# The second of two matrix products also made by Strassen's algorithm, summed over the tile, from the fourth tile on

## The chip, the cores and the metric

One core of one Trainium2 chip. The metric is the device time of one execution in microseconds, lower is better. The kernel before takes 828.13 us (median of 3 runs, 827.43 to 828.19). [...]

## The reference

Linear attention without softmax, then a norm, then a feed-forward network with the SiLU gate:

```
kv  = einsum('bhsd,bhse->bhde', k, v)              # 8 batches, 8 heads, 576 tokens, 64 dims
out = einsum('bhsd,bhde->bhse', q, kv)
x   = out / sqrt(mean(out*out, -1) + 1e-6) * g_norm # [8,8,576,64] -> tokens [4608, 512]
h   = x @ w_in                                      # [4608,512] @ [512,2048]
y   = (h * sigmoid(h)) @ w_out                      # [4608,2048] @ [2048,512]
```

All inputs are float32 (w_in and w_out reach the chip as 64-bit floats and are rounded there).

## The kernel before, in words

The 4608 tokens are cut into 9 **tiles** of TN = 512 tokens, counted here from 0 to 8. Each float32 operand of a product is split into an upper part (a cast to the PE's fp32r format) and a lower part (the difference), and a product is three products of parts: upper by lower, lower by upper, upper by upper. So a product has a *cast on ACT* and a *subtraction on DVE or POOL* ahead of it.

Tiles 0 and 1 run plainly, while the weights still arrive. From tile 2 on a tile is 8 **steps** i = 0 to 7 (`pair_step`), each with two blocks of 128 rows of the hidden dimension, i and i + 8:

- *First product* (x by w_in): Strassen's algorithm in Winograd's form. Seven products of 6 matmuls (128x256 each), called here by the numbers of the code: 1, 2, 6, 7, then 4, 5, 3. Products 1 and 2 share one PSUM bank (`bank`), 6 and 7 another (`other`); 4 and 5 go over 1 and 2, and 3 over 6. There are two such banks ("hp", pool `ps_h`). ACT copies product 1 (`p1`), DVE makes three sums from it (L706 to L708), then the results c2 (L718) and c1 (L722, L723).
- *Second product* (the gated block by w_out, `project`): plain. ACT runs SiLU twice on each result (once into the upper part gh), DVE subtracts (L667, gl), and the PE does 4 groups of 6 matmuls for each of the two blocks, 48 in all, growing four PSUM banks ("acc") over the whole tile. The PE runs it one step late, so that one step's gating lies beside the next step's first product.

The sums of blocks of w_in that Strassen's algorithm needs are made once in tile 1, kept in DRAM, and loaded anew in each step: two DMAs of 512 KB (`load_sums`), each issued when the PE has done with the block's predecessor. The operands made of x for the next tile are made in step 7 of a tile (`prepare` calls `make_operand`: 7 casts on ACT, L645, and 7 subtractions on DVE, L646): four of them stand ahead of c2 and c1 on DVE, three behind.

Beside this runs the attention of the next tiles' batches, one batch in a tile up to tile 6 (batches 3 to 7 in tiles 2 to 6), placed by tables (`first_jobs`, `mid_jobs`, `last_jobs`: ahead of, in the middle of and behind each half step): 80 small matmuls of k by v in step 7 (`mm_kv`), then in steps 0 and 1 of the next tile the splits of q (ACT L287, POOL L288) and of kv (`kh` on ACT, `kl` on DVE L280), and in steps 1 and 2 the products by q in two halves of 256 and 320 columns (`mm_out`: L301 to L303, between products 7 and 4 and behind product 3), which ACT reads twice (`copy_out`, L307 and L308). Two banks ("at" and "other") take turns for these halves. DVE scales (L321, L329) the batch before.

The schedule is manual: every engine's order is the order of the code. SP issues all DMAs in one queue.

## Time and profile before

| | |
|---|---|
| median of 3 runs | 828.13 us (827.43 to 828.19) |
| the profiled execution's own time | 827.72 us |
| its span on the core | 825.9 us, so 1.8 us lie outside it |
| granted TensorE clock | 1.00 in every stage |
| PE, DVE, ACT, POOL busy in the span | 815.1, 527.6, 358.4, 145.6 us |
| tiles 3, 4 and 5 | 87.6 us each |
| DMA moved | 122.81 MB, mean 149 GB/s |

The profile's page gives the busy time of each engine, the chain of work that ended last, and groups of instructions by line of the code with their mean duration; further views give the instructions in order of time and busy time by stretches of the span. A busy engine is not the bound by that alone: what counts is whether others wait for it.

### The profile page before, as it was taken

Reading aid. Unit: us, or ns where it says so; the run is one execution under the profiler, and the core shown is the slowest. Engines: PE = TensorE matmul, PEld = TensorE weight load, DVE = VectorE, ACT = ScalarE, POOL = GpSimd, SP = SyncE. Lnnn points to the kernel's source line nnn. Section 1 sums busy time; section 2 is a strip of 40 time slices with the busy share of each in tenths; the row PEclk is TensorE's granted clock in tenths of the full one; section 3 lists DMA queues with packets and bytes.
Section 4 is the critical chain, followed back from the end, with each engine's and each line's share of the span. In section 5 each row is a group of like instructions: output and inputs, shape, how many; then the busy total and the mean of one; then the engine's idle time right before and its main releaser. Section 6 shows DMA issues by size and latency. Waiting matters only on the chain.

```text
span 825.9 us, 18181 instructions
## 1 busy us (share of the span) xinstructions
PE 815.1 (99%) x7518; PEld 808.5 (98%) x7518; DVE 527.6 (64%) x1027; ACT 358.4 (43%) x744; POOL 145.6 (18%) x142
## 2 busy tenths in 40 slices
PE   8989999999999999999999999999999999999998
PEld 7889999999999999999999999999999999999998
DVE  4886884888476567757676668656765764464332
ACT  4766554534363255325442455225533423243222
POOL 2786883423020002000200011001100000000000
PEclk9999999999999999999999999999999999999999
DMA  8879011246352635364424453454423343334331
GB/s 324 321 245 380 7 42 70 102 182 233 126 177 95 218 120 169 103 214 149 168 77 163 161 182 103 143 177 160 143 92 104 108 159 106 106 106 155 103 103 52
DMA packets 42434, 122.81 MB, mean 149 GB/s; under 512 B 4848, under 2 KB 5104, under 8 KB 42352
## 3 DMA queue, kind: packets, MB, share of 16 engines
q1 hardware_dynamic: 42352, 121.65, 42.2%
q8 instruction: 59, 0.97, 0.5%
q14 instruction: 23, 0.19, 0.1%
HBM read 103.81 MB, written 17.83 MB: 147 GB/s over the span
## 4 chain that ended last, share of the span: by engine, by line
PE 94%; DMA 4%; POOL 1%; ACT 0%; issue 0%; SPq 0%
PE acc L488 46%; PE hp L654 32%; PE hp L488 9%; PE at L266 2%; DMA wo<-in_moe_w_out 1%; DMA k<-in_k 1%; DMA v<-in_v 1%; PE at L302 1%; PE at L303 1%; PE at L301 1%; DMA wi<-in_moe_w_in 1%; PE at L488 1%; DMA early_wi<-in_v 1%; PE at L299 1%; POOL wo L204 0%
## 5 line engine op out<-in xcount | busy, mean ns | idle before, releaser
L488 PE MATMUL acc<-wo,gh 128*128 128x256 f32 x2272 | 353.6, 277 | 0.0
L488 PEld LDWEIGHTS acc<-wo,gh 128*128 128x128 f32 x2272 | 302.1, 188 | 1.0 <-POOL wo L204 0.2
L488 PE MATMUL acc<-wo,gl 128*128 128x256 f32 x1136 | 222.9, 276 | 0.5 <-POOL gl L507 0.5
L488 PEld LDWEIGHTS acc<-wo,gl 128*128 128x128 f32 x1136 | 171.8, 188 | 0.7 <-POOL gl L507 0.7
L654 PE MATMUL hp<-x_second,wi 128*128 128x256 f32 x1344 | 163.1, 276 | 0.0
L654 PEld LDWEIGHTS hp<-x_second,wi 128*128 128x128 f32 x1344 | 157.2, 188 | 0.0
L654 PE MATMUL hp<-operand,wi 128*128 128x256 f32 x1008 | 123.3, 276 | 0.0
L654 PEld LDWEIGHTS hp<-operand,wi 128*128 128x128 f32 x1008 | 118.4, 188 | 0.0
L288 POOL TENSOR_TENSOR ql<-q,qh 128x576 fp32r<-128x576 f32 x24 | 35.3, 1472 | 368.2 <-ACT qh L287 321.7
L705 ACT COPY wi<-hp 128x256 f32<-128x256 f32 x56 | 20.8, 372 | 136.8 <-PE hp L654 136.8
L663 ACT ACTIVATE gh<-gf 128x512 fp32r<-128x512 f32 x56 | 35.4, 633 | 91.9 <-DVE gf L718 80.3
L663 ACT ACTIVATE gh<-wi 128x512 fp32r<-128x512 f32 x56 | 35.5, 634 | 76.6 <-DVE wi L718 66.3
L706 DVE TENSOR_TENSOR gf<-hp,wi 128x256 f32<-128x256 f32 x28 | 11.9, 425 | 81.6 <-ACT wi L705 81.6
L706 DVE TENSOR_TENSOR wi<-hp,wi 128x256 f32<-128x256 f32 x28 | 11.9, 425 | 81.2 <-ACT wi L705 81.2
L488 PE MATMUL hp<-x,wi 128*128 128x256 f32 x360 | 46.4, 283 | 1.4 <-POOL wi L204 1.4
L488 PE MATMUL hp<-x_second,wi 128*128 128x256 f32 x384 | 46.3, 276 | 0.0
L488 PEld LDWEIGHTS hp<-x,wi 128*128 128x128 f32 x360 | 43.5, 189 | 2.2 <-POOL wi L204 1.6
L667 DVE TENSOR_TENSOR gl<-wi,gh 128x512 fp32r<-128x512 f32 x56 | 38.4, 685 | 11.3 <-ACT wi L664 11.3
L488 PEld LDWEIGHTS hp<-x_second,wi 128*128 128x128 f32 x384 | 44.9, 188 | 0.1
L667 DVE TENSOR_TENSOR gl<-gf,gh 128x512 fp32r<-128x512 f32 x56 | 39.2, 700 | 7.4 <-ACT gf L664 7.4
L707 DVE TENSOR_TENSOR wi<-hp,wi 128x256 f32<-128x256 f32 x56 | 23.8, 425 | 29.5 <-PE hp L654 29.5
L307 ACT ACTIVATE sq<-at 128x256 f32<-128x256 f32 (+1 forms) x56 | 22.9, 410 | 44.5 <-PE at L303 35.7
(142 smaller groups left out, 1011.1 us busy)
## 6 DMA issues: line engine op xcount, KB each, us to landing
wi<-sums_in_dram SPq DMA_DIRECT2D x112, 512.0 KB, 3.3
out<-ob SPq DMA_DIRECT2D x35, 256.0 KB, 2.4
wi<-in_moe_w_in SPq DMA_DIRECT2D x16, 512.0 KB, 7.9
wo<-in_moe_w_out SPq DMA_DIRECT2D x16, 512.0 KB, 8.7
sums_in_dram<-sum_parts SPq DMA_DIRECT2D x16, 512.0 KB, 3.0
k<-in_k SPq DMA_DIRECT2D x28, 288.0 KB, 5.1
v<-in_v SPq DMA_DIRECT2D x28, 288.0 KB, 5.2
q<-in_q SPq DMA_DIRECT2D x28, 288.0 KB, 3.7
```

The lines of the kernel that those rows point to most:

```text
L266: nc.tensor.matmul(out=self.kv[h], lhsT=self.k[rows, c, :], rhs=self.v[rows, c, :], start=(start and r == 0), stop=(stop and r == 4),)
L288: nc.gpsimd.tensor_tensor(out=self.ql, in0=self.q, in1=self.qh.bitcast(F32), op=ALU.subtract)
L299: nc.tensor.matmul(out=ps, lhsT=self.kvm, rhs=self.q[:, w], start=True, stop=True)
L301: nc.tensor.matmul(out=ps, lhsT=self.kh, rhs=self.ql[:, w], start=True, stop=False)
L307: nc.scalar.activation(out=self.sq[:, self.w], in_=self.ps, func=AF.Square)
L488: nc.tensor.matmul(out=to[:, at:at + 256], lhsT=stationary, rhs=moving[:, at:at + 256], start=start and at == 0, stop=stop and at == n - 256,)
L654: nc.tensor.matmul(out=out, lhsT=a_of(i, a, c), rhs=x[:, b, c], start=(n == 0), stop=(n == 5))
L663: nc.scalar.activation(out=gh, in_=x, func=AF.Silu)
L667: nc.vector.tensor_tensor(out=gl, in0=x, in1=gh.bitcast(F32), op=ALU.subtract)
L705: nc.scalar.copy(out=p1, in_=u)
L706: nc.vector.tensor_tensor(out=c1[:, low], in0=v, in1=p1, op=ALU.add)
L707: nc.vector.tensor_tensor(out=u2, in0=y, in1=p1, op=ALU.add)
```

## The change

From tile 3 on (`SECOND = 3`) a step is `both_step`. The first product and its seven products are as before (now in `first_product`). The second product becomes seven products too, of 6 matmuls each (42 in place of 48), in the order 1, 5, 4, 6, 7, 3, 2. Both operands need sums of blocks:

- **w_out's sums**: eight jobs (`make_wo_sums`) in tile 2, each with two additions of 512 columns on POOL, four of 256 on DVE, two casts on ACT, two subtractions on POOL, and four DMAs into DRAM. Each step then loads four of 256 KB (`load_wo_sum`, rows of 1 KB) besides the two of 512 KB of w_in.
- **The gated block's sums**: ACT now runs SiLU once on c2 and c1. POOL makes three sums of 256 columns (s1, s2 and s3; it overwrites parts of c2). Then come the splits: a11|s3 (that is c2 now; cast on ACT, subtraction on DVE), s1|s2, a12|a22 (that is c1) and s4 (a further 256 on POOL) with the cast on ACT and the subtraction on POOL. Seven POOL instructions a step, where there was none. The subtraction of a11|s3 and the splits of a12|a22 and s4 run in the next step, between its products 7 and 4 (`between`, `flush_left`).
- **Where it is summed**: products 1 to 5 grow over the tile in five PSUM banks (four "acc" and "other"). Products 6 and 7 go to the two "hp" banks, alternating with the first product, and DVE adds each onto a sum in SBUF (`grown`).
- At a tile's end c11, c22, c21, c12 are put together from these by DVE, ACT and POOL, in steps 0 and 1 of the next tile, and stored in four DMAs of 256 KB.
- Since "other" is taken, the attention's halves have one bank ("at") from tile 2 on. Also, g_norm's factor moves from DVE's scaling (now `tensor_tensor`) into ACT's copy (L308), and the Newton steps of the norm get their scratch in the "at" bank.

The diff's core:

```
     def both_step(t, i, groups, before):
+        begin(g)
+        ... # c1, c2: places in turn
+        first_product(t, i, c1, c2, between)       # between: flush_lower(), flush_left()
+        run(left_late)
+        begin(g + 1)
+        if before is None:                          # tile 3, step 0: tile 2's plain rest
+            due(groups, 4); run(mid_jobs.pop(g + 1, ())); due(groups, len(groups)); move_b11(HF - 1)
+        s12 = place_out("units_sums", 3, F32)[:, 0]
+        for c in (c2, c1):
+            nc.scalar.activation(out=c, in_=c, func=AF.Silu)
+        nc.gpsimd.tensor_tensor(out=s12[:, 0], in0=c2[:, 1], in1=c1[:, 1], op=ALU.add)
+        subtract(nc.gpsimd, c2[:, 1], c2[:, 0], c2[:, 1])
+        subtract(nc.gpsimd, s12[:, 1], s12[:, 0], c2[:, 0])
+        def make_a11_s3():
+            upper, lower = gated["a11_s3"]
+            nc.scalar.copy(out=upper, in_=c2)
+            left.insert(0, lambda: subtract(nc.vector, lower, c2, upper.bitcast(F32)))
+        def make_s4():
+            subtract(nc.gpsimd, s12[:, 0], c1[:, 0], s12[:, 1])
+            make([gated["s4"][:, a] for a in range(2)], s12[:, 0], nc.gpsimd)
+        def make_a12_a22():
+            make(gated["a12_a22"], c1, nc.gpsimd)
+        ...
+        second_products(*before, {                  # what is issued behind which product
+            5: [lambda: load_wo_sum(i, 1)],
+            4: [lambda: load_wo_sum(i, 4), jobs(mid_jobs)],
+            6: [lambda: load_wo_sum(i, 2)],
+            7: [lambda: load_wo_sum(i, 3), make_a11_s3, make_s12],
+            3: [jobs(last_jobs)],
+        })
+        left[1:1] = [make_a12_a22, make_s4]
+    def second_products(t, i, after):
+        for m in (1, 5, 4, 6, 7, 3, 2):
+            bank = second_product(t, i, m)          # 6 matmuls; m < 6 grows, 6 and 7 take an "hp" bank
+            if m > 5 and i == 0:
+                nc.vector.tensor_copy(out=sums[m], in_=...)
+            elif m > 5:
+                add(sums[m], bank, sums[m])
+            ...                                     # at i == 7: c11, c22, c21, c12
+            for call in after.get(m, ()):
+                call()
     def at_bank(tag=None):
+        if tag == "at" and "at" in once:
+            return once["at"]
     def copy_out(self):
-            nc.scalar.copy(out=self.o[:, self.w], in_=self.ps)
+            nc.scalar.activation(out=self.o[:, self.w], in_=self.ps, func=AF.Copy, scale=gcol)
     def scale(self, segment):
-            nc.vector.scalar_tensor_tensor(out=to, in0=self.o[:, a:e], scalar=gcol, in1=self.yT, op0=ALU.mult, op1=ALU.mult)
+            nc.vector.tensor_tensor(out=to, in0=self.o[:, a:e], in1=self.yT, op=ALU.mult)
```

Three places show how the instructions move.

ACT in step 1 of tile 6, from the copy p1 (L705 before, L695 now) to the last read of the first attention pair's halves (sq and o). Before:

```order
L705 COPY wi_3112<-hp 128x256
L307 ACTIVATE sq<-at 128x256
L308 COPY o<-at 128x256
L287 CAST qh<-q 128x576
L307 ACTIVATE sq<-at 128x320
L308 COPY o<-at 128x320
```

Now (L952: the upper parts of a12|a22 and of s4; L881: c21's copy):

```order
L695 COPY wi_3112<-hp 128x256
L952 CAST gh<-wi_4370 128x512
L952 CAST gf<-wo_4503 128x256
L881 COPY ob<-acc 128x512
L308 ACTIVATE sq<-at 128x256
L309 ACTIVATE o<-at,gcol 128x256
L288 CAST qh<-q 128x576
L308 ACTIVATE sq<-at 128x320
L309 ACTIVATE o<-at,gcol 128x320
```

Three instructions moved ahead of the first half's read, and the second of them reads what POOL has made of s4.

ACT in step 7 of tile 6, from p1 to the SiLU (L663 before, L945 now), with the casts of the next tile's operands (L645, now L646). Before:

```order
L705 COPY wi_3112<-hp 128x256
L645 CAST operand_2921<-x_0_1925 128x512
L645 CAST operand_2925<-x_1_2097 128x512
L645 CAST operand_2960<-t_8552 128x512
L645 CAST x_second<-x_0_1925 128x512
L645 CAST x_second<-t_8553 128x512
L645 CAST x_second<-t_8551 128x512
L645 CAST x_second<-x_1_2097 128x512
L663 ACTIVATE gh<-wi_3112 128x512
```

Now:

```order
L695 COPY wi_3112<-hp 128x256
L952 CAST gh<-wi_4370 128x512
L952 CAST gf<-wo_4503 128x256
L646 CAST operand_2922<-x_0_1926 128x512
L646 CAST operand_2926<-x_1_2098 128x512
L646 CAST operand_2961<-t_8846 128x512
L646 CAST x_second<-x_0_1926 128x512
L646 CAST x_second<-t_8847 128x512
L646 CAST x_second<-t_8845 128x512
L646 CAST x_second<-x_1_2098 128x512
L945 ACTIVATE wo_4503<-wo_4503 128x512
```

The seven casts stand behind the cast of s4 now.

POOL, before, from tile 1's last work to the end of the program (L288 is the split of q):

```order
L204 TENSOR_TENSOR wo_1824<-wo_full,wo_1824 128x512
L288 TENSOR_TENSOR ql<-q,qh 128x576 x3
L563 TENSOR_TENSOR sum_parts<-sums,sum_parts 128x512
L288 TENSOR_TENSOR ql<-q,qh 128x576
L563 TENSOR_TENSOR sum_parts<-sums,sum_parts 128x512 x15
L288 TENSOR_TENSOR ql<-q,qh 128x576 x20
```

Now, in steps 0 and 1 of tile 5 (L955 and L948: the sums and lower parts; L846: c21's sum):

```order
L955 TENSOR_TENSOR wo_4503<-wi_4370 128x256
L948 TENSOR_TENSOR wi_4370<-wi_4370 128x256
L948 TENSOR_TENSOR wo_4503<-wo_4503,wi_4370 128x256
L289 TENSOR_TENSOR ql<-q,qh 128x576
L948 TENSOR_TENSOR gl<-wo_4503,gh 128x512
L948 TENSOR_TENSOR gl<-wi_4370,gh 128x512
L948 TENSOR_TENSOR wo_4503<-wi_4370,wo_4503 128x256
L948 TENSOR_TENSOR gf<-wo_4503,gf 128x256
L846 TENSOR_TENSOR ob<-ob,wo_4616 128x512
L289 TENSOR_TENSOR ql<-q,qh 128x576
```

Where a tile had only its four splits of q, each now stands between the gated block's sums.

More of the change, by code (lines that the diff above doesn't have):

```diff
@@ L453, in rsqrt @@
         else:
[L454 removed]
+            if "at" in once:
+                m, u = (once["at"][:, at:at + n] for at in (S - 256, S - 256 + n))
+            else:
+                m, u = (small.tile([P, n], F32, name=name, bufs=1) for name in ("m", "u"))
             calls = [
@@ L510, in gate, with sums_of, project @@
         return gh, gl
[L512 to L521 removed]
+    def sums_of():
+        return [(acc_bank(), n) for n in range(TN // P)]
+    def project(t, f, gh, gl, bank, n):
         first, last = order(t)[0], order(t)[-1]
@@ new lines, in second_product @@
+    def second_product(t, i, m):
+        if m == 1 and i == 0:
+            accs.update({n: acc_bank() for n in (1, 2, 3, 4)})
+            accs[5] = at_bank("other")
+        grown = m < 6
+        bank = accs[m] if grown else h_bank()
+        begins, ends = i == 0 or not grown, i == HF - 1 or not grown
+        g, w = gated[m], of_out(i, m)
+        for k, (a, b) in enumerate(((0, 1), (1, 0), (0, 0))):
+            for n in range(2):
+                nc.tensor.matmul(
+                    out=bank[:, n * H:(n + 1) * H], lhsT=g[a][:, n * P:(n + 1) * P], rhs=w[:, b],
+                    start=begins and k == 0 and n == 0, stop=ends and k == 2 and n == 1,
+                )
+        return bank
@@ new lines, in add, with store, out_tile @@
+    def add(to, x, y, engine=None):
+        (engine or nc.vector).tensor_tensor(
+            out=to, in0=x.rearrange("p (a n) -> p a n", a=2) if len(x.shape) == 2 else x, in1=y, op=ALU.add
+        )
+    def store(t, row, half, ob):
+        rows = slice(t * TN + row * H, t * TN + (row + 1) * H)
+        nc.sync.dma_start(out=out[rows, (low, high)[half]].rearrange("(n p) c -> p n c", p=P), in_=ob)
+    def out_tile():
+        return tmp.tile([P, S], F32, name="ob", tag="tmp")[:, :TN].rearrange("p (a n) -> p a n", a=2)
```

241 lines of the change are left out of this document (192 added, 49 removed).

## The prediction

> **What bounds the kernel now.** First the page's busy times and the line shares of the chain that ended last, then the busy times by stretches.
>
> ```profile
> span 825.9 us, 18181 instructions
> PE 815.1 (99%) x7518; PEld 808.5 (98%) x7518; DVE 527.6 (64%) x1027; ACT 358.4 (43%) x744; POOL 145.6 (18%) x142
> PE acc L488 46%; PE hp L654 32%; PE hp L488 9%; PE at L266 2%; DMA wo<-in_moe_w_out 1%; DMA k<-in_k 1%; DMA v<-in_v 1%; PE at L302 1%; PE at L303 1%; PE at L301 1%; DMA wi<-in_moe_w_in 1%; PE at L488 1%; DMA early_wi<-in_v 1%; PE at L299 1%
> core 0: us, PE busy (x) PEld busy (x) DVE busy (x) ACT busy (x) POOL busy (x), PEclk, DMA share, GB/s
> 394.10:481.70 87.60, 87.60 (x826) 87.34 (x825) 58.75 (x120) 37.79 (x81) 5.72 (x4) 1.00 0.44 149
> 656.90:735.90 79.00, 79.00 (x700) 79.00 (x699) 44.52 (x84) 27.35 (x48) 0.00 (x0) 1.00 0.36 121
> ```
>
> The PE is the bound: tile 4 (394.1 to 481.7) and about tile 7 (656.9 to 735.9) have no gap, at clock 1.00. So fewer matmuls count in full, and so does every new gap. In tile 4 DVE is at 58.75 of 87.60; POOL is empty. The chain in order of time prices a block:
>
> ```profile
> 350.63 4.76 PE hp L654 x42
> 355.39 5.44 PE acc L488 x48
> 360.83 4.76 PE hp L654 x42
> ```
>
> A matmul costs 5.44/48 = 0.1133 us, a Strassen product of six 0.68, a step 10.20.
>
> **What the change removes.** Six matmuls a step, 8 steps, 6 tiles: 288 x 0.1133 = 32.6 us. A step without attention becomes 9.52 us.
>
> **What it adds, in a step.** Seven POOL instructions. Rows by shape:
>
> ```profile
> L204 POOL TENSOR_TENSOR wo<-wo_full,wo 128x512 fp32r<-128x512 f32 x16 | 20.8, 1300 | 4.1 <-ACT wo L203 4.1
> L439 POOL TENSOR_TENSOR x_second<-xf,x_second 128x256 fp32r<-128x256 f32 x1 | 0.8, 752 | 0.0
> L288 POOL TENSOR_TENSOR ql<-q,qh 128x576 fp32r<-128x576 f32 x24 | 35.3, 1472 | 368.2 <-ACT qh L287 321.7
> ```
>
> Five of 256 columns and two of 512: 5 x 0.75 + 2 x 1.30 = 6.35 us of 9.52. In steps 0 and 1 two splits of q (2.9) join, in step 1 also c21's sum (1.3). The second cost is in the instructions in order of time, where DVE meets POOL:
>
> ```profile
> 571.94 1.43 POOL L288 TENSOR_TENSOR ql<-q,qh 128x576 fp32r<-128x576 f32 x1 [68.96 <-ACT qh L287]
> 572.23 0.42 DVE L707 TENSOR_TENSOR wi<-hp,wi 128x256 f32<-128x256 f32 x1 [0.53 <-PE hp L654]
> 573.02 0.90 DVE L667 TENSOR_TENSOR gl<-gf,gh 128x512 fp32r<-128x512 f32 x1
> 115.79 1.30 POOL L204 TENSOR_TENSOR wo<-wo_full,wo 128x512 fp32r<-128x512 f32 x1
> 115.97 1.60 DVE L329 SCALAR_TENSOR_TENSOR o<-o,gcol,yT 128x448 f32<-128x448 f32 x1
> 117.03 1.68 POOL L507 TENSOR_TENSOR gl<-gf,gh 128x512 fp32r<-128x512 f32 x1
> ```
>
> L707, which reads one operand from PSUM, runs its 0.42 beside POOL. L667, with both in SBUF, ends at 573.92, 0.55 behind POOL's end at 573.37. L329 waited likewise until 117.09 and ended at 117.57; POOL's next came after it (1.68 for 1.30). So two SBUF-to-SBUF instructions of DVE and POOL exclude each other and take turns. [...] Were that only a slowing in proportion, the turns' share of the terms below (1.5 in step 0, an estimated 1 in each step 1, 0.5 in each step 7: 7 in all) would go and the sum be about 813; the rows show whole instructions waited for.
>
> *A plain step*, from its first matmul, with step 7 of tile 3 for the unchanged head:
>
> ```profile
> 381.07 2.20 PE L654 MATMUL hp<-operand,wi 128*128 128x256 f32 x18
> 382.63 0.37 ACT L705 COPY wi<-hp 128x256 f32<-128x256 f32 x1 [3.01 <-PE hp L654]
> 382.90 1.14 ACT L645 CAST operand<-x 128x512 fp32r<-128x512 f32 x2
> 384.79 0.68 DVE L667 TENSOR_TENSOR gl<-wi,gh 128x512 fp32r<-128x512 f32 x1
> 385.93 2.70 PE L266 MATMUL at<-v,k 128*64 128x64 f32 x80
> 387.20 0.68 DVE L646 TENSOR_TENSOR x_second<-x,x_second 128x512 fp32r<-128x512 f32 x1
> 387.80 0.68 DVE L718 TENSOR_TENSOR wi<-hp,wi 128x512 f32<-128x512 f32 x1
> 388.40 0.41 DVE L722 TENSOR_TENSOR gf<-hp,wi 128x256 f32<-128x256 f32 x1
> 390.46 0.68 DVE L646 TENSOR_TENSOR x_second<-x,x_second 128x512 fp32r<-128x512 f32 x1
> ```
>
> p1 ends at 1.93; the cast of a12|a22 at 2.6 (0.62; a second one 0.52 behind, from 1.14 for two); POOL's lower part 2.6 to 3.9; DVE's lower part of a11|s3, free at 3.7, ends at 4.47; POOL's s4 5.1, its cast 5.5, its lower part 6.3; the two SiLUs end at 6.85; three POOL sums 9.1; the lower part of s1|s2 at 1.6 of the next step. The PE wants a11|s3's lower part at 4.76 + 0.23 = 4.99 (spare 0.5), the others later; POOL is free 0.6 before its next work. So a plain step costs nothing, hidden by the first product's 4.76; the upper end is 0.3 a step. The sums on DVE of products 6 and 7 (0.68 each, L718) lie beside products 7, 3 and 2.
>
> *Step 7 (tiles 3 to 7)*. Its operand casts now stand behind s4's cast, which ends at 5.5 as above, or 6.1 since the sums of x at the end of step 6 (four of 0.68, SBUF to SBUF) take a turn from POOL; they started at 1.83 before. DVE makes four lower parts (0.60 apart, 387.20 to 387.80) ahead of c2 and c1: the first is ready for at 6.7 but gives POOL a turn, the fourth ends near 9.3, c1's first add at 10.3 (7.7 in the row of 388.40). Product 6 needs that bank at 6.8, where before the next use of it came 5.44 us of matmuls later. So in tiles 6 and 7 the PE waits about 3.5 there; four products on it is at 13.0, and the next tile's first matmul needs product 6's sum, which DVE makes behind three more lower parts: 13.35, so 3.8 late. From 2.5 (no turn lost) to 4.4 (each lost), taken 3.5: 7.0 for two. In tiles 3, 4, 5 the attention's small matmuls (2.7) cover most: 0 to 1.8, taken 1.0: 3.0.
>
> *Step 0 (tiles 4 to 6)*: kl and the scaling wait for POOL's turns ahead of product 6's sum: 0 to 1.4, taken 0.5: 1.5.
>
> *The halves, steps 1 and 2*, one bank now:
>
> ```profile
> 506.63 0.28 PE L303 MATMUL at<-qh,kh 128*128 128x256 f32 x1
> 506.95 0.38 ACT L307 ACTIVATE sq<-at 128x256 f32<-128x256 f32 x1 [1.33 <-PE at L303]
> 507.23 0.37 ACT L308 COPY o<-at 128x256 f32<-128x256 f32 x1
> 508.79 0.30 PE L301 MATMUL at<-ql,kh 128*128 128x320 f32 x1
> ```
>
> The first half's bank is read by 507.60, the second half starts at 508.79: spare 1.2 on an idle ACT. Now ACT first waits for s4 (POOL, 4.7 to 5.9 into the step), casts it, in step 1 copies c21, then reads: done at 6.4 to 7.5 in step 1, against 5.1 on the PE. And c1's first sum there stands behind a kl that waits for POOL: product 4 waits 0 to 1.3. Together 1.3 to 2.5, taken 2.0, three tiles: 6.0. Step 2 has no c21: 0.7 in tiles 3 to 6: 2.8; tile 3's step 1: 0.7.
>
> *Tile 2*: w_out's sums, 41.6 us on POOL (32 x 1.30) and 13.4 on DVE (32 x 0.42), under a plain second product with 5.44 of cover: 0 to 8, taken 1.0.
>
> *The end*:
>
> ```profile
> 822.58 0.28 PE L488 MATMUL at<-wo,gl 128*128 128x256 f32 x1
> 822.89 0.37 ACT L530 COPY ob<-at 128x256 f32<-128x256 f32 x1 [0.31 <-PE at L488]
> ```
>
> The last seven products follow their gating with no first product between: s1|s2 at 11.15 where product 5 wants it at 10.43, then a12|a22: 1.45 of waits. The last sum takes 0.68 for 0.37 and stores 256 KB for 128: 0.8. Together 2.2.
>
> *DMA*: 1 MB more a step, in 1 KB rows.
>
> ```profile
> GB/s 324 321 245 380 7 42 70 102 182 233 126 177 95 218 120 169 103 214 149 168 77 163 161 182 103 143 177 160 143 92 104 108 159 106 106 106 155 103 103 52
> wi<-sums_in_dram SPq DMA_DIRECT2D x112, 512.0 KB, 3.3
> out<-ob SPq DMA_DIRECT2D x35, 256.0 KB, 2.4
> ```
>
> 149 GB/s in tile 4 becomes about 270, under the 380 of the fourth slice; a load has 8.8 us from free to needed and such sizes land in 2.4 to 3.3. On SP, step 1's loads stand behind c21's store, which waits for POOL (8.2 into the step); they land near 12, needed near 15. Cost 0.
>
> Sum: 7.0 + 3.0 + 1.5 + 6.0 + 2.8 + 0.7 + 1.0 + 2.2 = 24.2 given back of 32.6; 8.4 remain. 827.72 - 8.4 = 819.3; the median is 0.4 above the profiled execution: 819.7. The lower ends sum to 14.6 (810); the upper ends, without tile 2's and the plain steps', to 31.6 (827).
>
> **The rivals.**
>
> *Nearly all is hidden*: if DVE is served ahead of POOL and the casts are on time, only the end's 2.2 and little else stays: 798 to 808. For it: the plain step fits. Against: step 7's order on ACT and DVE. 0.13.
>
> *Slower: the turns make DVE the bound of tiles 3 to 6.* DVE there: 58.75 - 16 lower parts x 0.69 + 8 x 0.69 + 16 sums x 0.68 + the tile's end 4.1 - 1.4 = 66.8 us. 32 of its instructions are SBUF-to-SBUF (8 lower parts, 8 scalings, 7 operands, 4 sums of x, 4 kl, 1 at the end). The tile's PE is 87.6 - 5.44 = 82.2. The waits seen above are 0.21 (0.90 - 0.69) and 0.91 (1.60 - 0.69). At 0.48 each DVE fills the tile; with tiles 7 and 8 gaining 10.9 - 7.0 and the end losing 2.2, the kernel becomes slower from about 0.66. At 0.75: 90.8 a tile, 4 x 3.2 - 1.7 = 11 more: 839. Against: POOL would be busy 58 of 82 us (8 x 6.35 + 4 x 1.47 + 1.3), and a wait lasts half an instruction of 0.75 to 1.47 on the mean, so 0.71 x 0.52 = 0.37. 0.20.
>
> *DMA becomes the bound.* Laid end to end a step's loads are 4 x 2.4 + 2 x 3.3 = 16.2 us against 9.52; 47 such steps would add over 300: about 1130. The page's 380 GB/s speaks against it, 0.03. [...]
>
> **How the numbers follow.** Forecast 0.60 (810 to 826), hidden 0.13, slower 0.20, DMA 0.03, within the 0.2% (1.7 us) that a measurement can tell 0.04. Faster 0.73, same 0.04, slower 0.23. The range leaves out half of the hidden case, the slower case's end and the DMA: 802 to 836.
>
> **What would show it.** PE waits in step 7 for DVE's adds on hp; PE waits at L302 for ACT's copy o; DVE subtractions lengthened to 1 us and more; POOL at 70% in tiles 3 to 8; tile 7's step 7 near 13 us, plain steps at 9.52. Wrong if plain steps are longer than 9.6, or the PE waits for a load.

## The result, and the profile after

The changed kernel takes 858.7 us (median of 4 runs, 858.0 to 861.4), the kernel before 827.96 beside it: a ratio of 1.0378 (1.0355 to 1.0402). It is 30.7 us slower, where 8.4 us faster was forecast. The profiled execution took 858.0 us, its span 856.2. The rows call TensorE PE, VectorE DVE, ScalarE ACT, GpSimd POOL and SyncE SP. First the page's busy times, then the busy times by stretches: tile 2, tile 4, and tile 7.

```profile
span 856.2 us, 18904 instructions
PE 805.2 (94%) x7230; PEld 790.9 (92%) x7230; DVE 613.0 (72%) x1132; ACT 409.7 (48%) x858; POOL 526.0 (61%) x515
219.70:320.00 100.30, 91.47 (x827) 90.01 (x825) 79.20 (x154) 49.43 (x102) 49.78 (x36) 0.98 0.63 214
409.50:497.70 88.20, 84.44 (x779) 83.00 (x778) 69.44 (x133) 44.27 (x97) 62.12 (x62) 1.00 0.74 244
676.60:761.90 85.30, 79.43 (x672) 78.50 (x672) 55.27 (x98) 33.95 (x66) 57.54 (x58) 1.00 0.66 210
```

The PE has 288 matmuls fewer, as planned (7518 to 7230), but it waits in every tile. The start of each tile's first matmul in the two traces gives what each tile lost against its matmuls alone (its length before, less 0.1133 us for each matmul removed):

| | measured | matmuls alone | lost | forecast |
|---|---|---|---|---|
| start to tile 2 | | | 0.7 | 0 |
| tile 2 | 100.3 | 87.6 | 12.8 | 1.0 |
| tile 3 | 89.9 | 82.8 | 7.1 | 2.4 |
| tile 4 | 88.2 | 82.2 | 6.0 | 4.2 |
| tile 5 | 89.6 | 82.2 | 7.4 | 4.2 |
| tile 6 | 88.9 | 79.3 | 9.6 | 6.7 |
| tile 7 | 85.3 | 76.2 | 9.1 | 3.5 |
| tile 8 and its end | | | 10.2 | 2.2 |
| sum | | | 62.9 | 24.2 |

62.9 less 32.6 saved is 30.3, the difference of the spans. So the saving is there, and two and a half times the forecast loss. Three kinds of loss show, of which the forecast had only the first.

*Waits.* The instructions in order of time, with the wait and its releaser in brackets: the longest in tile 2, tile 4's, step 7 of tiles 6 and 7, one load:

```profile
237.05 2.27 PE L655 MATMUL hp<-x_second,wi 128*128 128x256 f32 x13 [3.97 <-DVE gf L696]
424.80 2.33 PE L655 MATMUL hp<-x_second,wi 128*128 128x256 f32 x18 [0.88 <-DVE wi L696]
428.37 0.41 PE L302 MATMUL at<-ql,kh 128*128 128x320 f32 x1 [1.25 <-ACT o L309]
440.92 0.42 PE L302 MATMUL at<-ql,kh 128*128 128x320 f32 x1 [0.79 <-ACT o L309]
673.20 0.47 PE L839 MATMUL hp<-wo,gh 128*128 128x256 f32 x2 [3.04 <-issue]
758.48 0.47 PE L839 MATMUL hp<-wo,gh 128*128 128x256 f32 x2 [2.53 <-issue]
784.61 0.94 PE L655 MATMUL hp<-operand,wi 128*128 128x256 f32 x6 [1.24 <-DMA wi<-sums_in_dram]
```

L696 is c1's first sum (L707 before), L309 the read of an attention half, L839 the second product. The two waits put down to "issue" are product 6's for its bank: DVE's add on that bank (L710, from 757.98, 0.41 long) ends 0.1 ahead of 758.48.

*Half a clock.* A stretch of 3.4 us right behind the first wait, and the next one:

```profile
238.10:241.50 3.40, 3.40 (x18) 3.40 (x17) 3.10 (x6) 0.27 (x1) 3.40 (x3) 0.50 0.99 303
241.60:245.00 3.40, 3.40 (x32) 3.40 (x31) 2.52 (x7) 2.89 (x8) 0.67 (x1) 1.00 0.39 139
```

The granted clock (third column from the end) is 0.50, and 18 matmuls pass instead of some 30: 1.4 us. The same follows tile 3's first long wait (2.88 us at 336.29): the granted clock is 0.50 from 337.1 to 340.5.

*A wider spacing.* Steps with no wait at all, in tile 3 and in tile 7:

```profile
368.29 2.20 PE L655 MATMUL hp<-operand,wi 128*128 128x256 f32 x18
377.81 2.20 PE L655 MATMUL hp<-operand,wi 128*128 128x256 f32 x18
709.15 2.28 PE L655 MATMUL hp<-operand,wi 128*128 128x256 f32 x18
719.04 2.28 PE L655 MATMUL hp<-operand,wi 128*128 128x256 f32 x18
```

The first pair is 9.52 us apart, as forecast. The second is 9.89 apart with the clock at 1.00: 18 matmuls take 2.28 for 2.20, so they stand 117.9 ns apart instead of 113.3. This spacing stays for tens of us (in tile 5 from 529.7 to 579.7, 425 matmuls in 50 us), then goes. Summed over the trace it costs about 8 us; the kernel before shows 0.2.

The end: behind the last matmul (its row covers two, to 848.75) DVE still has six additions, then the store:

```profile
848.36 0.39 PE L839 MATMUL acc<-wo,gh 128*128 128x256 f32 x2
848.87 0.69 DVE L846 TENSOR_TENSOR wo<-wo 128x512 f32<-128x512 f32 x1
849.59 0.69 DVE L846 TENSOR_TENSOR ob<-acc,wo 128x512 f32<-128x512 f32 x1
850.20 0.68 DVE L846 TENSOR_TENSOR ob<-at,wo 128x512 f32<-128x512 f32 x1
850.80 0.68 DVE L846 TENSOR_TENSOR wo<-at,wo 128x512 f32<-128x512 f32 x1
851.57 0.69 DVE L846 TENSOR_TENSOR ob<-acc,wo 128x512 f32<-128x512 f32 x1
852.18 0.68 DVE L846 TENSOR_TENSOR ob<-acc,ob 128x512 f32<-128x512 f32 x1
```

From the last matmul to the end of the span it is 7.45 us; before, 3.08.

### The profile page after: what moved, and what is told of

It is laid out like the page before. It is cut to its first block, busy times and chain, and to the rows that moved or that the text cites. A ratio compares the mean times of both kernels' runs of the same rounds, so it can differ in the third digit from the quotient of the medians.

```text
span 856.2 us, 18904 instructions
## 1 busy us (share of the span) xinstructions
PE 805.2 (94%) x7230; PEld 790.9 (92%) x7230; DVE 613.0 (72%) x1132; ACT 409.7 (48%) x858; POOL 526.0 (61%) x515
## 5 line engine op out<-in xcount | busy, mean ns | idle before, releaser
L495 PE MATMUL acc<-wo,gh 128*128 128x256 f32 x768 | 120.7, 279 | 0.0
L839 PE MATMUL acc<-wo,gh 128*128 128x256 f32 x576 | 113.5, 279 | 0.0
L495 PEld LDWEIGHTS acc<-wo,gh 128*128 128x128 f32 x768 | 102.9, 189 | 0.8 <-POOL wo L205 0.2
L839 PEld LDWEIGHTS acc<-wo,gh 128*128 128x128 f32 x576 | 87.8, 188 | 0.2
L948 POOL TENSOR_TENSOR gl<-wo,gh 128x512 fp32r<-128x512 f32 x48 | 63.9, 1332 | 31.9 <-ACT gh L952 31.9
L952 ACT CAST gf<-wo 128x256 fp32r<-128x256 f32 x48 | 19.5, 407 | 130.2 <-POOL wo L948 130.2
L846 DVE TENSOR_TENSOR wo<-hp,wo 128x512 f32<-128x512 f32 x84 | 56.6, 686 | 34.5 <-PE hp L839 34.1
L948 POOL TENSOR_TENSOR gl<-wi,gh 128x512 fp32r<-128x512 f32 x48 | 62.1, 1295 | 29.3 <-ACT gh L952 29.3
L696 DVE TENSOR_TENSOR wi<-hp,wi 128x256 f32<-128x256 f32 x52 | 22.0, 423 | 79.2 <-ACT wi L695 78.9
L495 PE MATMUL acc<-wo,gl 128*128 128x256 f32 x384 | 75.4, 278 | 0.5 <-POOL gl L514 0.5
L839 PE MATMUL hp<-wo,gh 128*128 128x256 f32 x384 | 68.2, 280 | 8.0 <-issue 7.3
L839 PEld LDWEIGHTS hp<-wo,gh 128*128 128x128 f32 x384 | 54.8, 188 | 8.9 <-issue 7.9
L495 PEld LDWEIGHTS acc<-wo,gl 128*128 128x128 f32 x384 | 58.1, 188 | 0.7 <-POOL gl L514 0.7
L948 POOL TENSOR_TENSOR wo<-wi,wo 128x256 f32<-128x256 f32 x48 | 58.6, 1220 | 0.0
L839 PE MATMUL acc<-wo,gl 128*128 128x256 f32 x288 | 56.9, 279 | 0.3 <-POOL gl L948 0.3
L948 POOL TENSOR_TENSOR gf<-wo,gf 128x256 fp32r<-128x256 f32 x48 | 35.6, 742 | 24.8 <-ACT gf L952 24.8
L945 ACT ACTIVATE wi<-wi 128x512 f32<-128x512 f32 x72 | 44.2, 630 | 9.7 <-DVE wi L707 5.6
```

The costliest lines, as they stand in the source:

```text
L495: nc.tensor.matmul(out=to[:, at:at + 256], lhsT=stationary, rhs=moving[:, at:at + 256], start=start and at == 0, stop=stop and at == n - 256,)
L696: nc.vector.tensor_tensor(out=c1[:, 0], in0=v, in1=p1, op=ALU.add)
L839: nc.tensor.matmul(out=bank[:, n * H:(n + 1) * H], lhsT=g[a][:, n * P:(n + 1) * P], rhs=w[:, b], start=begins and k == 0 and n == 0, stop= ...
L846: (engine or nc.vector).tensor_tensor(out=to, in0=x.rearrange("p (a n) -> p a n", a=2) if len(x.shape) == 2 else x, in1=y, op=ALU.add)
L945: nc.scalar.activation(out=c, in_=c, func=AF.Silu)
L948: engine.tensor_tensor(out=to, in0=x, in1=y, op=ALU.subtract)
```

## The experiments

Theories at the start: **A**, the loss is waits, made by POOL and DVE taking turns and by where the new work stands in the queues; **B**, the engines beside the PE have too little room, so that a wait taken away comes back elsewhere; **C**, the PE itself runs slower after stalls.

### Does a stall cost more than itself?

The kernel before, with one stall in each of tiles 2 to 8 (e4):

```
         product(6, i, y)
+        nc.scalar.copy(out=p1, in_=u)
+        for _ in range(STALLS[t] if i == 3 else 0):   # 3, 5, 7, 9, 12, 15, 20
+            nc.scalar.copy(out=z, in_=u)
         product(7, i, z)
-        nc.scalar.copy(out=p1, in_=u)
```

> The kernel before with one artificial stall of the PE in step 3 of each of tiles 2 to 8: ACT makes 3, 5, 7, 9, 12, 15 and 20 copies from product 1's bank into product 7's, and product 7 waits for them; estimated stalls 0.2, 0.75, 1.3, 1.85, 2.7, 3.5 and 4.9 us, 15.2 in all. If a stall costs only itself: 841 to 845, and matmuls stay 113.3 ns apart. If a stall can leave the PE at 117.9 ns until the next one, tiles behind such stalls take up to 3.5 us more each: 848 to 865. If waits of about 2.9 us and more halve the granted clock for 3.4 us, the last two or three stalls cost 1.7 more each.

Measured: 870.5 us, ratio 1.0529 (1.0501 to 1.0556). The copies took longer than estimated; the stalls were 1.22, 2.00, 2.78, 3.55, 4.72, 5.88 and 7.82 us, 28.0 in all. The spans differ by 43.1, so 15 us came on top. The stretches behind the stalls (the first two behind 2.78 and 3.55; then 20 us of tile 6 and of tile 7):

```profile
437.90:441.30 3.40, 3.40 (x18) 3.40 (x18) 2.16 (x5) 0.00 (x0) 0.00 (x0) 0.50 0.44 154
530.10:533.50 3.40, 3.39 (x16) 3.39 (x17) 1.86 (x4) 0.00 (x0) 0.00 (x0) 0.50 0.21 55
650.00:670.00 20.00, 20.00 (x172) 20.00 (x171) 11.05 (x25) 6.13 (x11) 0.00 (x0) 1.00 0.32 106
740.00:760.00 20.00, 20.00 (x178) 20.00 (x178) 10.48 (x20) 5.50 (x10) 0.00 (x0) 1.00 0.33 107
```

Each stall from 2.78 us on is followed by half a clock, for 3.4 us, and for 6.8 (partly within the stall) at the two longest; 1.22 and 2.00 are not. Tile 6 ran at the wide spacing from its stall to the next one (172 matmuls in 20 us), tile 7 at the narrow one again (178). Tile 5 ran wide behind its stall (two matmuls in 0.40 us at 535.02) and narrow again ahead of the next one (18 in 2.20 at 618.98), with no stall in between. C holds as an addition to the waits. The length of a wait alone does not tell whether half a clock follows: the 3.04 at 673.20 above went unpunished (clock 1.00 from 672 to 690), but behind waits of 2.78 us here, and of 1.76 and 2.04 in e1, the matmuls ran at half the pace (in e1 two take 0.63 us for 0.40 at 695.99, and 18 take 3.63 for 2.20 at 520.64).

The changed kernel profiled once more, unchanged (e16):

> The changed kernel once more, unchanged. If the spacing of 117.9 ns belongs to the program: the same stretches as in the first profile show it (tile 5 from its third step on, most of tiles 7 and 8). If it belongs to the execution: other stretches. The waits themselves stand where they were, to 0.1 us.

It took 860.83 us. The waits stand where they were, to 0.3 us. The same two stretches of 40 us, first in the first profiled execution, then in the second:

```profile
360.00:400.00 40.00, 40.00 (x355) 40.00 (x354) 30.25 (x67) 15.77 (x30) 27.70 (x29) 1.00 0.80 271
540.00:580.00 40.00, 40.00 (x341) 39.90 (x339) 28.91 (x65) 14.97 (x28) 28.09 (x29) 1.00 0.82 276
360.00:400.00 40.00, 40.00 (x342) 40.00 (x341) 29.63 (x65) 14.85 (x28) 26.58 (x27) 1.00 0.80 268
540.00:580.00 40.00, 40.00 (x355) 40.00 (x355) 30.10 (x68) 15.59 (x30) 28.27 (x29) 1.00 0.79 270
```

The slow and the fast stretch have changed places: the spacing belongs to the execution, not to the program. What sets it stays open.

### Is it POOL and DVE together?

The changed kernel with POOL's seven instructions a step cut to 32 columns, from the second step of tile 3 on (e13):

```
+            if engine is nc.gpsimd:
+                to, x, y = (a[..., w] for a in (to, x, y))
             engine.tensor_tensor(out=to, in0=x, in1=y, op=ALU.subtract)
         ...
-        nc.gpsimd.tensor_tensor(out=s12[:, 0], in0=c2[:, 1], in1=c1[:, 1], op=ALU.add)
+        w = slice(0, H if before is None else 32)
+        nc.gpsimd.tensor_tensor(out=s12[:, 0, w], in0=c2[:, 1, w], in1=c1[:, 1, w], op=ALU.add)
```

> The changed kernel with POOL's seven instructions a step cut to 32 columns each from tile 3's second step on (the other columns are left out; order, waits and all else as they are). Theory A (POOL and DVE are one resource for SBUF-to-SBUF work: in a tile POOL's 58 us and DVE's 32 instructions of 0.69 make 80 of the 82 us of matmuls, in step 7 6.35 + 8 x 0.69 = 11.9 of 9.5): nearly all waits of tiles 3 to 8 go, some 20 to 25 us with their half clocks: 833 to 840. Theory B (ACT's and DVE's order, whatever POOL's pace): the waits at the halves and in step 7 stay above half of what they are: 846 to 853.

837.8 us, ratio 1.0107 (1.0093 to 1.0122): 20.9 less than the change. Tile 4 and tile 7 now, and DVE's lower parts and kl in tile 4, first in the changed kernel, then here:

```profile
411.40:496.40 85.00, 84.76 (x779) 84.19 (x778) 64.13 (x132) 44.50 (x98) 22.98 (x61) 1.00 0.77 253
664.50:744.30 79.80, 77.53 (x673) 76.73 (x672) 52.44 (x98) 34.28 (x66) 17.51 (x57) 1.00 0.71 225
L281 DVE TENSOR_TENSOR kl<-kvm,kh 128x128 fp32r<-128x128 f32 x4 | 4.6, 1142 | 0.8 <-ACT kh L280 0.8
L948 DVE TENSOR_TENSOR gl<-wo,gh 128x512 fp32r<-128x512 f32 x4 | 3.6, 892 | 0.0
L281 DVE TENSOR_TENSOR kl<-kvm,kh 128x128 fp32r<-128x128 f32 x4 | 1.1, 281 | 0.0
L950 DVE TENSOR_TENSOR gl<-wo,gh 128x512 fp32r<-128x512 f32 x4 | 2.7, 681 | 0.0
```

With the order untouched, tiles 4 to 8 with the end lost 21 us, where they had lost 42. A kl of 0.28 us had taken 1.14. The waits at the halves of tiles 4 to 6 are gone although they still have one bank, so the single bank alone does not make them. POOL's time is the largest single part of the loss. But this run shortens two things at once, the turns that DVE loses and the chains that run through POOL itself (ACT's wait for s4, see the halves below). How much belongs to each is not shown.

The counter-test puts the same amount of POOL work into the kernel before, where nothing waits for it (e9):

```
         upper_part(c2, hi[0])
+        for n in (H, H, H, TN, TN, H, H) if t >= 3 else ():
+            x = hi[0].bitcast(F32)[:, :n]
+            nc.gpsimd.tensor_tensor(out=..., in0=x, in1=x, op=ALU.add)   # out: a place that nothing reads
```

> The kernel before with idle work on POOL: in each step of tiles 3 to 8 seven additions from SBUF to SBUF (five of 256 columns, two of 512, as the change has them), which read an upper part and write a place that nothing reads. Theory A (POOL and DVE take turns, and only that): DVE's two subtractions a step grow from 0.69 to 1.0 to 1.8 us, the PE waits only in step 7, where seven stand together, up to 1 us a tile: 828 to 834. Theory B (POOL's work slows the rest by itself, the reads of PSUM or the PE too): each step loses some tenths: 840 or more. Theory C (the turns cost nothing, the change's loss is all in the order of its own new work): 828 to 829 and no new wait.

831.12 us, ratio 1.0032 (1.0021 to 1.0043). In tile 4 DVE's two subtractions a step grew to 818 and 734 ns, not to 1000 and more, and DVE's busy time from 58.75 to 63.13 us. The only waits are of 0.23 us, in step 4 of tiles 3 to 6, for c1's sum behind the norm's small instructions. So turns beside work that nothing waits for cost 3 us; how much of that is wide spacing is not shown. In step 7 the four subtractions ahead of c2 hardly meet POOL here (0.68 us each in tiles 3, 6 and 7), so this run says nothing of the change's step 7. An estimate from the rows: POOL's 52.4 us in tile 4 here and DVE's 39 SBUF-to-SBUF instructions, some 23, make 75 of 87.6; in the change POOL's 58 (62.1 measured, with its waits in it) and DVE's some 18 make 76 of 82.2, and in step 7 6.35 + 8 x 0.68 = 11.8 of 9.52. The two kernels differ in more than this sum, since in the change the PE also waits for the chain through both engines.

### Tile 2

One of the eight jobs of w_out's sums, the rest left out (e3):

```
-        for i, third in enumerate((2, 7, 12, 17, 23, 27, 32, 37)):
+        for i, third in enumerate((2,)):
```

> The changed kernel with one of the eight jobs of w_out's sums in tile 2; every step loads the sums of that one, so seven eighths of those sums are left out and nothing else. If these sums cost tile 2 its time: its PE waits of 3.97, 1.69, 1.25 and 1.44 us (8.7 in all), the first one's half clock (1.7) and a part of the waits in step 0 of tile 3 go: 846 to 850. If tile 2's waits come of the single bank for the attention's halves, the 3.97 alone goes or nothing: 854 to 858.

850.98 us, ratio 1.0277 (1.0261 to 1.0293): 7.7 less. The waits of 1.69, 1.25 and 1.44 are gone; the 3.97 with its half clock stays, since the job that stayed is the first one, at the same place. The rows behind that wait in the changed kernel show that it begins with a wait for a buffer:

```profile
232.73 0.38 DVE L322 STREAM_TRANSPOSE yT<-y 128x192 f32<-128x192 f32 x1 [1.89 <-DMA out<-ob]
233.58 0.59 ACT L531 COPY ob<-acc 128x512 f32<-128x512 f32 x1 [2.52 <-DVE x L330]
236.17 0.37 ACT L695 COPY wi<-hp 128x256 f32<-128x256 f32 x1
236.57 0.42 DVE L696 TENSOR_TENSOR gf<-hp,wi 128x256 f32<-128x256 f32 x1
```

By the code, yT takes one of five shared buffers (pool `tmp`), and the job takes two of them for its rows. Here yT waits until a result is stored; before the change it ran at 229.80 without a wait. ACT's copy of the next result waits for the scaling behind yT, and p1 (L695) stands behind that copy and the job's two casts: 236.17, for 230.90 before. c1's sum (L696) and the PE follow. No run gives the job buffers of its own, so the buffer's share of the 3.97 us is not shown. Then all eight, moved (e6):

> The changed kernel with the eight jobs of w_out's sums moved: the first to the end of tile 1, the other seven into steps 2 to 7 of tile 2, behind most of the attention's halves; the work is the same. If tile 2's waits (3.97 us, with half a clock behind it, then 1.69, 1.25, 1.44) come of where the jobs stand in ACT's and DVE's order: they shrink to 3 us or less in all and the time is 849 to 853. If the work itself is too much for DVE, ACT and POOL in tile 2, the waits come back at other places: 857 to 861.

860.21, no gain: two waits of 3.49 and 5.41 us took the place of five. The first of them:

```profile
277.30 1.47 DVE L786 TENSOR_TENSOR first_rows<-first_rows 128x256 f32<-128x256 f32 x1 [1.18 <-POOL first_rows L783]
280.14 0.42 DVE L696 TENSOR_TENSOR gf<-hp,wi 128x256 f32<-128x256 f32 x1
280.61 1.74 PE L655 MATMUL hp<-x_second,wi 128*128 128x256 f32 x9 [3.49 <-DVE gf L696]
```

DVE's first sum of a job waits for POOL's addition and then lasts 1.47 for 0.42, and c1's sum, for which the PE waits, stands behind it in DVE's queue. B was right here: the place is moved, the crowd is not.

### Step 7

Only ACT's order put back (the casts of operands 1, 2, 6, 7 ahead of s4's; e2):

> The changed kernel with one edit in step 7: the casts of the next tile's operands 1, 2, 6 and 7 stand on ACT ahead of the casts of a12|a22 and s4, as they did before the change; DVE's order is as it is. If ACT's order is what makes product 6 wait in step 7: its waits of 3.0 (tile 6) and 2.5 us (tile 7) go below 1 and those of tiles 3 to 5 (0.4 to 0.8) vanish, 6 us in all: 851 to 853. If DVE's four subtractions lose their time to POOL's turns, whatever ACT does, the waits stay above 2: 857 to 859. If a12|a22 and s4 come too late instead, products 4 and 3 wait up to 1.5 in six tiles: 858 or more.

855.57 us, ratio 1.0340 (1.0313 to 1.0366). Product 6 still waits 2.53 in tiles 6 and 7, as the second forecast said, so putting ACT's order back gained 0.5 of the 3.04 in tile 6 and nothing in tile 7. Of the rest of its 3.1 us, some 2 are spacing in the two traces: tile 7 takes 83.3 us here and 85.3 in the change, with the same waits, and runs narrow here (18 matmuls in 2.20 us at 707.20 and 716.72). The rows of the changed kernel, in tile 6, show that ACT's order was a cause all the same:

```profile
668.60 0.41 ACT L952 CAST gf<-wo 128x256 fp32r<-128x256 f32 x1 [2.94 <-POOL wo L948]
669.56 1.41 DVE L647 TENSOR_TENSOR operand<-x,operand 128x512 fp32r<-128x512 f32 x2 [1.60 <-ACT operand L646]
672.70 0.41 DVE L710 TENSOR_TENSOR wi<-hp,wi 128x256 f32<-128x256 f32 x1
```

ACT waits for POOL's s4, DVE for the first operand's cast behind that; the four subtractions then take about 0.7 us each, and c1's sum stands behind them. With the casts first (e2) the subtractions start 4.3 us into the step instead of 6.4, but now they meet POOL and the first three take 1.2 us each. Either cause alone holds product 6 up. Then DVE's order as well, with only one subtraction ahead of c2 (e7):

> The changed kernel with another order in step 7: the operand casts 1, 2, 6, 7 ahead of s4's cast on ACT, and on DVE only one of the operand subtractions ahead of c2, the others spread behind c2, c1 and the additions of products 6 and 7. If the four subtractions ahead of c2 make product 6 wait: the waits of 3.0 and 2.5 us in tiles 6 and 7 and of 0.4 to 0.8 in tiles 3 to 5 go, 6 to 8 us: 850 to 853. If DVE is simply full in step 7 (subtractions, sums and turns fill the 9.5 us), the wait moves to the first product of the next tile: 857 to 860.

861.38, no gain. Product 6 no longer waits, and the first product of the next tile does, for c1's sum behind the subtractions that were put off (tile 8; L709 is that sum here):

```profile
764.62 1.95 DVE L647 TENSOR_TENSOR x_second<-t,x_second 128x512 fp32r<-128x512 f32 x2 [2.73 <-ACT x_second L646]
766.50 0.68 DVE L647 TENSOR_TENSOR x_second<-x,x_second 128x512 fp32r<-128x512 f32 x1
767.10 0.41 DVE L709 TENSOR_TENSOR wi<-hp,wi 128x256 f32<-128x256 f32 x1
767.56 3.38 PE L668 MATMUL hp<-x_second,wi 128*128 128x256 f32 x18 [2.62 <-DVE wi L709]
```

The work has to leave the step; that is tried last.

### The halves

s4's cast on POOL, so that ACT doesn't wait for it (e1):

```
-            make([gated["s4"][:, a] for a in range(2)], s12[:, 0], nc.gpsimd)
+            upper, lower = (gated["s4"][:, a] for a in range(2))
+            nc.gpsimd.tensor_copy(out=upper, in_=s12[:, 0])      # s4's cast, on POOL
+            subtract(nc.gpsimd, lower, s12[:, 0], upper.bitcast(F32))
```

> The changed kernel with one edit: the cast of s4 runs on POOL (0.75 us more a step there) in place of ACT, so that ACT never waits for POOL between the seven sums and the attention's reads. Theory A (ACT's order behind POOL costs the time): the PE's waits of 1.24 and 0.88 us at the attention's halves (tiles 3 to 6, 7.3 us in all) go below 0.3 each, and in step 7 the operand casts start about 3 us earlier, so that the 3.0 and 2.5 us before product 6 of tiles 6 and 7 shrink below 1: 846 to 851 us. Theory B (POOL's turns with DVE cost it): POOL is busy 36 us longer, the subtractions on DVE wait more, 857 or slower. Theory C (the PE's own pace after stalls costs it): with fewer stalls the spacing of 117.9 ns gives way to 113.3, some 3 to 5 us beyond the waits that go: 842 to 847.

852.05 us, ratio 1.0273 (1.0238 to 1.0307): 6.7 less. In the changed kernel ACT waited 3.65 for s4 ahead of the first half's read, and the second half for that; here the second half of step 1's first pair starts on time, but a wait comes back one pair later, since ACT finds no free buffer while results are being stored:

```profile
426.78 0.41 ACT L952 CAST gf<-wo 128x256 fp32r<-128x256 f32 x1 [3.65 <-POOL wo L948]
431.32 0.39 ACT L308 ACTIVATE sq<-at 128x256 f32<-128x256 f32 x1 [2.93 <-DMA out<-ob]
432.12 0.42 PE L302 MATMUL at<-ql,kh 128*128 128x320 f32 x1 [1.69 <-ACT o L309]
```

(The first row is of the changed kernel, the others of this one.) Both A and B are seen in three lines: the wait for s4 is gone, and another comes back. In step 7 product 6 still waits 2.54 and 2.03, where this run's theory A had said below 1.

### The end

The last step's products in the order 1, 7, 5, 6, 4, 3, 2 (e5):

> The changed kernel with the last step's seven second products in the order 1, 7, 5, 6, 4, 3, 2 in place of 1, 5, 4, 6, 7, 3, 2, so that DVE's sums of products 6 and 7 no longer stand behind the last but two. Theory: the end costs 7.45 us from the last matmul to the end of the span (3.04 before the change) because six additions of 0.69 on DVE, not one, stand behind product 7: now two stand behind the last product, 4.1 to 4.6 us, 2.5 to 3.3 us off the whole: 855 to 856. If the store is what takes the time, the end stays at 7 us: 858 to 859.

862.69 us, ratio 1.0414 (1.0397 to 1.0432), a miss. The end shrank from 7.45 to 6.3 only, and product 7 now waited 1.91 for its w_out sum, which is loaded last. Behind the sum of product 6 seven additions still follow, not two.

### All repairs, and a smaller change

All repairs with the moved jobs and the new step 7 (e8), and then without the moved jobs and with DVE's order of step 7 as in the change, the two that had gained nothing alone (left are s4's cast behind the half's read, casts first in step 7, tile 3's first splits behind p1, c21 on DVE, the stores of c22 and c21 behind the load, and another order of the last step; most of these were not tried alone; e10):

> All repairs in one kernel: the jobs of w_out's sums moved, step 7's order, the last step's order, s4's cast behind the first attention half's reads on ACT, SiLU of tile 3's step 0 ahead of the result copies and its first splits behind p1, c21 summed on DVE straight from PSUM, and the stores of c22 and c21 behind the next load on SP. Theory A (the time lost is waits that ACT's, DVE's and SP's order makes): 7 + 5 + 6 + 3 + 9 us go, with about 3 us of half clocks: 823 to 831. Theory B (the engines beside the PE have too little room, so a wait taken away comes back further on): 840 to 850. Theory C (spacing of 117.9 ns after stalls, whatever they are): of 858.7 some 5 to 8 us stay in any version that has stalls at all.

> The changed kernel with the repairs that helped: the operand casts first on ACT in step 7 (DVE's order as in the change), s4's cast behind the first attention half's reads, SiLU of tile 3's step 0 early and its splits behind p1, c21 on DVE, the stores of c22 and c21 behind the load, and the last step's order 1, 5, 7, 6, 4, 3, 2; w_out's sums where the change has them. If the waits add up as they stand in the traces: against 852.97 with the other step 7 and the moved jobs, 1.4 less at each of five tile ends and 1 to 2 at the last step: 844 to 848. If waits only change places: 851 to 855.

852.97 (ratio 1.0305, 1.0278 to 1.0333) and 843.01 (1.0194, 1.0166 to 1.0221). The first lies above both forecast ranges; in its trace the first product of tiles 4 to 8 waits 2.2 to 2.7 us, as in e7, and tile 2 has waits of 3.26 and 4.87, as in e6, which is theory B's picture. The second lies 1 us below its first forecast, that the waits add up. Tile 2 is untouched in it, and tile 2 of its trace is still 14.5 us longer than before the change.

The change on tiles 7 and 8 alone, with the jobs two a tile in tiles 2 to 5 (e11); then with those repairs (e12):

```
-    SECOND = 3
+    SECOND = 7
-        for i, third in enumerate((2, 7, 12, 17, 23, 27, 32, 37)):
-            spread_out(lambda i=i: make_wo_sums(i), 3 * 2 * NF + third, 2, 0, 4, 1, 1)
+        for i in range(HF):
+            spread_out(lambda i=i: make_wo_sums(i), 3 * (2 + i // 2) * NF + (20, 30)[i % 2], 2, 0, 4, 1, 1)
```

> The change from the eighth tile on only (tiles 7 and 8, which have no attention of their own): the second product of tiles 3 to 6 stays plain with two banks for the halves, and the jobs of w_out's sums are spread over tiles 2 to 5, two a tile. 10.9 us of matmuls go. If the loss is the crowd of waits of tiles 2 to 6: left are the first splits of the new form (3.0 and a half clock of 1.7), step 7 of tile 7 (3.2), the load in tile 8 (1.4) and the end (4.9), 14 us: 829 to 833. If w_out's sums cost the same wherever they stand: 8 to 10 more, 838 to 842. If waits in tiles 7 and 8 were hidden by nothing but luck before: above 842.

> The same from tile 7 on, with the repairs: the first splits behind p1 and SiLU ahead of the result copies, operand casts first in step 7, c21 on DVE, the stores behind the load, and the last step's order. If waits add up: the 3.0 and its half clock, the load's 1.4 and about 1 of the end go: 822 to 827, faster than the kernel before. If waits only change places: 829 to 833.

864.99 (1.0435, 1.0412 to 1.0458) and 855.60 (1.0333, 1.0308 to 1.0358). The first is above 842, as its third forecast said, but both are slower than the waits of tiles 7 and 8 can make them, and the second is above both of its forecasts. In both, each of tiles 2 to 5 has one wait of 3.44 us, at the end of its first job. Half clocks come on top (the mean granted clock of the two profiled executions is 0.980 and 0.989, for 1.000 before), though none right behind the wait in tile 2 of the second (13 matmuls in 1.74 us at 269.53). DVE's c1 sum, for which the PE waits, stands behind four tiny copies of the norm, here in tile 2 of the repaired kernel and then in tile 4 of the changed kernel, where they write into PSUM:

```profile
L458 DVE COPY m<-sums 32x72 f32<-32x72 f32 x4 | 4.8, 1211 | 0.1
L458 DVE COPY at<-sums 32x72 f32<-32x72 f32 x4 | 0.9, 232 | 0.1
```

SBUF to SBUF, each waits for a whole instruction of POOL: the four take 4.88 us from 262.95 on, beside four of POOL's of 1.26 to 1.34, and in tile 4 of the kernel before, with POOL nearly idle, such a copy takes 190 ns. With the jobs moved off them (e14), thirds (27, 35) in place of (20, 30), where a third is a place in the tables, three to a half step:

> The kernel repaired from tile 7 on (855.6), with the jobs of w_out's sums in tiles 2 to 5 moved from thirds 20 and 30 of a tile to 27 and 35, behind the four copies of the norm (32x72, SBUF to SBUF), which took 4.88 us together while POOL added beside them. If those turns are the 3.6 us a tile: four waits of 3.6 and the half clocks behind them (6 us) go: 832 to 837, less if fewer spells of 117.9 ns. If the jobs cost the same anywhere: 853 to 857.

834.46 us, ratio 1.0075 (1.0054 to 1.0096): 21 less, as forecast, and tiles 2 to 5 are 87.6 to 87.9 us in the profiled execution, its fastest (829.68). So w_out's sums cost next to nothing when spread. Last, four of the seven subtractions are taken out of step 7 of tile 7 (e15):

```
+        for m, third in ((1, -24), (2, -21), (7, -18), (6, -15)):   # made in steps 4 and 5
+            spread_out(lambda m=m: [lambda: make_early(m)], last + third, 1)
```

> As the one with the jobs moved off the norm, and the last tile's operands 1, 2, 6 and 7 are made in steps 3 to 6 of tile 7, into places that the attention has left, so that step 7 has three subtractions in place of seven. If step 7's 2.7 us come of seven subtractions and POOL's 6.35 us sharing 9.5: that wait and its half clock go: 3.5 to 4.5 faster than without it, 826 to 832. If product 6 waits there for the adds of c2 and c1 whatever stands ahead of them: no change.

830.09 us, ratio 1.0028 (1.0014 to 1.0042). The 2.53 at product 6 is gone (the kernel without this edit has it, at 734.01), and 1.15 at the place of the new subtractions came. Its runs lie at 827.9 to 829.0, 831.2 to 831.9 and 833.4 to 833.9: steps of about 3 us, by estimate what a tile at the wide spacing costs (80 us x 4.6 / 113). Only the slowest, 833.85, has a trace, and it runs wide at 668.80 (18 matmuls in 2.28 us) and at 819.15 (two in 0.40), and narrow at 679.73 and 730.01 (18 in 2.20). This is the best version, and it does not beat the kernel before.

## Why the prediction was wrong

The saving (32.6) was right, and so was the reading that DVE and POOL exclude each other (in tile 4 kl takes 1.14 us, and 0.28 where POOL's instructions are cut, e13). The plain step is at 9.52 where the spacing is narrow; at the wide one it is 9.89, above the 9.6 that the prediction named as a sign of being wrong, and once the PE waited for a load, the other sign. In that step's sum the lower part of a11|s3 ends at 4.40 by its rows (384.79 + 0.68 - 381.07), not at 4.47; nothing hangs on the difference. By its steps:

- *Step 7*: taken 3.5 in tiles 6 and 7; the waits there measured 3.04 + 0.37 and 2.53 + 0.46. Right, with the named chain: casts behind s4's, then four subtractions ahead of c1. What it did not see: with early casts the subtractions meet POOL instead (e2), so that only taking them out of the step helps (e15).
- *The halves*: taken 2.0 in step 1 and 0.7 in step 2; measured 0.88 + 1.25 and 0.79 in tile 4. Right, by the named chain.
- *Tile 2*: taken 1.0 out of 0 to 8, measured 12.8. This is the step that failed most. It set POOL's 41.6 us against the cover of a plain second product and asked how much work there is, not what stands behind it: c1's sum waits in DVE's queue behind the jobs' sums, which wait for POOL (e6), and p1 on ACT behind their casts; at the first job the buffers run short as well. One wait of 3.97 us and its half clock come of the first job alone (e3).
- *The end*: taken 2.2, measured 4.4 for additions and store, beside short waits. It counted the last sum, where six additions stand in DVE's queue when the last matmul starts.
- *DMA*: taken 0, measured 1.24 once. Such loads land in 3.8 us there (the median from 764 to 786 us); it was issued late on SP, behind a store that waited for POOL.
- *Left out altogether*: half clocks behind long waits, the wider spacing (about 8 us in the profiled execution), tile 3's first splits (2.88 and half a clock), and tile 7's step 1 (1.78 + 1.02), where DVE's sums stand behind scalings that wait for POOL.
- *The slower rival* had the right sign and was given 0.20, but its mechanism did not come: DVE, which it made the bound of tiles 3 to 6, is busy 69.4 of 88.2 us in tile 4. Its price was the turns in DVE's sum alone, 66.8 of 82.2 us, which looks roomy. Both engines' SBUF-to-SBUF work in one sum, 76 of 82.2, and 11.8 of 9.52 in step 7, looks tight; that this sum is the limit is argued, not shown. e13 puts the price of POOL's part at 20.9 us, which with the 7.7 of tile 2's later jobs (e3) makes 28.6 of the 30.7, if they add; the two were not tried together. The rest, and what remains in e13, are the first job's wait, the end, and stretches of half clock and wide spacing.

## What to carry to other kernels

When PE work is traded for work on DVE and POOL, add up the SBUF-to-SBUF instructions of both as one resource, stage by stage: they took turns here (kl 1.14 us for 0.28), 86% with nothing waiting for POOL cost 0.5 us a tile, and 92% with the PE waiting on the chain through both cost 6; where between them, or in the chain, the limit lies is not shown. Count also the shared buffers that new work takes. For each new instruction ask what stands behind it in its queue and who waits for that: taking one such wait away mostly uncovered the next. On a kernel that never let the PE stop, a stall can cost more than itself (in e4 stalls of 28.0 us cost 43.1): price 1.4 us or more for the half clock that may follow a wait of 2 to 4 us, and up to 3 us a tile for the wider spacing that may follow.

## What the runs showed of the hardware

- Half a clock for 3.4 us (the changed kernel, 238.1 to 241.5 and 337.1 to 340.5), or for some 6.8 (e4, from 714.4 and from 806.6), can come with a wait: one of 1.76 us was enough in e1, while one of 2.00 goes without in e4 (24 matmuls in 3.00 us at 346.39). In one program, the changed kernel, product 6's wait of 2.53 in tile 7 went without in one execution (clock 1.00 from 755 to 775) and was followed by half the pace in another (e16: two matmuls take 0.63 us at 763.93 for 0.40): what counts is not the length alone.
- Matmuls of 256 columns run 113.3 or 117.9 ns apart at a clock of 1.00 (the changed kernel, 18 in 2.20 us at 368.29 and in 2.28 at 709.15). The spacing holds over tens of us and changes at stalls (e4, tiles 5 to 7), but not only there: in tile 5 of the changed kernel it went back to the narrow one at step 7's 80 matmuls of 64 columns (two of 256 columns take 0.40 us at 574.76, ahead of them, and 0.39 from 583.24 on), and in tile 7 it began with no wait in sight (0.39 at 706.04, 0.40 at 706.56). It differs between executions of one program (e16: 342 matmuls in the 40 us from 360, for 355). Its cause is open.
- POOL's turn hits even a DVE copy of 32x72 with one input, SBUF to SBUF: 1211 ns beside POOL (e12, tile 2) for 190 in tile 4 of the kernel before. With its output in PSUM the copy takes 232 ns in tile 4 of the changed kernel, where POOL is busy 62.12 of 88.20 us.
